# Two MLPs behind an attention: the first MLP's last eight output products as seven quarter products, and its scale and offset applied behind them

## The chip, the cores and the metric

The kernel runs on one core of a Trainium2 chip. The metric is device time in microseconds: before, the median of three runs is 846.16 (846.07 to 846.45).

## The reference

Sparse attention over 4 sequences of 576 tokens and 8 heads of 64 gives x of 2304 tokens by 512. Two MLPs follow, each of width 2048. All is float32, and the second MLP has its own weights.

```python
# first MLP                       # second MLP
h = x @ w_in                      h = x @ w_in
r = np.maximum(h, 0.0)            g = where(h >= 1, h, where(h <= -1, 0, (h + 1)**2 / 4))
g = s * (r * r) + b               out = g @ w_out
out = g @ w_out                   # s and b are one number each
```

## The kernel before

**Engines.** PE is TensorE (matmuls), DVE is VectorE, ACT is ScalarE, POOL is GpSimd, SP is SyncE, which issues nearly all the DMAs.

**Number format.** Each float32 matrix is split into a high and a low part (fp32r), and each product is three matmuls: high by high, high by low, low by high (`mm3` at L698 to L700, `mm3s` at L948 to L950). The high part is a copy on ACT (`copy`, L311), the low part a subtraction on DVE. Weights arrive as 64-bit floats, 128 rows of 512 numbers (0.52 MB) each, and `decode` turns them to float32: one ACT step (L329) and two DVE steps (L331, L333).

**First MLP.** The tokens are six units of 384 (`UNITS`), the width 16 blocks of 128 (index g). `hidden(g, u)` makes one block for one unit: 12 matmuls into PSUM tile `h` (two of them), relu on ACT (L720), square on ACT or DVE (L724, L726), s and b (`affine`: DVE at L733, ACT at L731), the high part `gh` (L311) and the low part `gl` (L737). Two steps later `output(u, g)` adds this block's share to four accumulators `acc0..3` in 12 more matmuls. A step is thus 24 matmuls of 384 columns. The list `segments` first goes through blocks 0 to 7 for all units; their sums are stored to DRAM (`part_d`). Then blocks 8 to 15 follow unit by unit, and the last addition (L775) adds the stored half and leaves x2, the second MLP's input. The attention of later tokens runs between the steps of units 0 to 4. Unit 5 with blocks 0 to 7 ends at about 283 us, the first MLP at about 491 us.

**Second MLP.** Pairs of units are multiplied by seven products of quarters (`PRODS`) in place of eight; `SUMS` lists the sums of token quarters, T1 to T4, and the matching sums S1 to S4 of weight quarters are made beforehand by `prepare(o, i)`: two blocks decoded, four sums (L392), the seven quarters split (L311, L377) and stored to DRAM as `dw` (eight stores, on SP). There are 16 such calls, each once. `inputs(p)` makes the sums and splits of a pair's x2 (L815, L834); `hidden2(p)` and `output2(p)` hold the matmuls, six to a block, and load one 262 KB quarter of weights (`wmat`, L871) per block.

**Order of the work.** `Issue.order` plans it: each operation has a duration by engine, its dependencies and a due time worked backward from the end. The planner always starts what can start first, then what is due first, and every engine runs its operations in that order. A tag with a count (`buf`) is a ring of buffers: an operation that needs one waits for the oldest to be free. The planner prices a DMA by `DMA_RATE`, 390 GB/s.

## Time and profile before

| | |
|---|---|
| median of three runs | 846.16 us |
| profiled execution | 847.01 us |
| its span, first to last instruction | 845.2 us |
| around the span | 1.8 us |
| mean granted TensorE clock | 0.983 |

A page shows one profiled execution. The busy share of PE is that of pipelined matmuls whose shown durations overlap, so its rate is read from the count of matmuls in a stretch. "Idle before" in a group of instructions says how long the engine stood before them and what ended it; it costs time only where that engine's work is on the chain that ended last.

### The profile page before, as it was taken

To read this page: it belongs to the slowest core of one execution; us is meant where nothing else is said; L and a number is where in the kernel's file an instruction comes from. 1 tells how busy PE (TensorE), PEld (TensorE's weight loads), DVE (VectorE), ACT (ScalarE), POOL (GpSimd) and SP (SyncE) were. 2 spreads that over 40 slices of the span, in tenths; PEclk is the share of its full clock that TensorE was granted. 3 is DMA by queue.
4 is the path that set the end of the run, shared out by engine and by line. 5 is a ranking of instruction groups with operands and counts; after the bars stand their busy time and mean duration, and the time that the engine had idled before them with its cause. 6 is when DMAs were issued, how large, how long until landed. Compare 5 with 4: busy or idle time off the path is not lost.

```text
span 845.2 us, 17439 instructions
## 1 busy us (share of the span) xinstructions
PE 822.4 (97%) x6338; PEld 799.1 (95%) x6338; DVE 595.7 (70%) x1247; ACT 519.3 (61%) x1093; POOL 22.9 (3%) x68
## 2 busy tenths in 40 slices
PE   7699999999999999999999999999999999999998
PEld 4479998989999899999999999999999999999998
DVE  3679637475698885767778356897666998465966
ACT  5467645554576774556667467875477855577653
POOL 2110000010000000000001000000000000000000
PEclk8689999999999999999999999999999999999999
DMA  8959272363389993768786457888987889888883
GB/s 245 270 172 287 98 241 66 92 181 108 122 283 329 293 304 128 226 220 259 261 293 203 151 181 244 264 254 267 290 275 254 254 252 289 293 252 253 254 263 105
DMA packets 115931, 191.78 MB, mean 227 GB/s; under 512 B 13830, under 2 KB 57990, under 8 KB 115846
## 3 DMA queue, kind: packets, MB, share of 16 engines
q1 hardware_dynamic: 114818, 190.23, 71.1%
q8 instruction: 51, 0.84, 0.4%
q10 hardware_dynamic: 1028, 0.43, 0.2%
q14 instruction: 34, 0.28, 0.1%
HBM read 150.25 MB, written 40.37 MB: 226 GB/s over the span
## 4 chain that ended last, share of the span: by engine, by line
PE 83%; DMA 9%; DVE 4%; ACT 2%; issue 2%; SPq 0%; ACTq 0%; DVEq 0%
PE h L698 6%; PE h L699 6%; PE acc L698 6%; PE h L700 6%; PE acc L699 6%; PE acc L700 6%; PE acc L949 6%; PE acc L948 6%; PE acc L950 6%; PE side L949 5%; PE side L948 5%; PE side L950 5%; DMA raw<-in_w_ins 4%; PE h L949 3%; PE h L950 3%; PE h L948 3%
## 5 line engine op out<-in xcount | busy, mean ns | idle before, releaser
L720 ACT ACTIVATE t<-h 128x384 f32<-128x384 f32 x96 | 46.5, 484 | 57.8 <-PE h L700 57.5
L698 PE MATMUL acc<-gh,w1hx 128*128 128x384 f32 x192 | 65.3, 340 | 0.4 <-ACT gh L311 0.4
L698 PE MATMUL h<-xh,w0hx 128*128 128x384 f32 x192 | 65.1, 339 | 0.0
L699 PE MATMUL acc<-gl,w1hx 128*128 128x384 f32 x192 | 64.9, 338 | 0.3
L699 PE MATMUL h<-xl,w0hx 128*128 128x384 f32 x192 | 64.5, 336 | 0.0
L700 PE MATMUL acc<-gh,w1lx 128*128 128x384 f32 x192 | 64.5, 336 | 0.0
L700 PE MATMUL h<-xh,w0lx 128*128 128x384 f32 x192 | 64.2, 334 | 0.0
L311 ACT ACTIVATE gh<-t 128x384 fp32r<-128x384 f32 x96 | 50.0, 520 | 23.0 <-DVE t L733 22.5
L737 DVE TENSOR_TENSOR gl<-t,gh 128x384 fp32r<-128x384 f32 x93 | 51.6, 555 | 16.4 <-ACT gh L311 16.2
L733 DVE TENSOR_SCALAR t<-t,fix_t 128x384 f32<-128x384 f32 x79 | 37.7, 477 | 35.2 <-ACT t L724 34.9
L698 PE MATMUL acc<-gh,w1h 128*128 128x384 f32 x168 | 57.0, 339 | 0.0
L699 PE MATMUL acc<-gl,w1h 128*128 128x384 f32 x168 | 56.4, 336 | 0.0
L700 PE MATMUL acc<-gh,w1l 128*128 128x384 f32 x168 | 56.3, 335 | 0.0
L698 PE MATMUL h<-xh,w0h 128*128 128x384 f32 x144 | 50.3, 349 | 0.1
L699 PE MATMUL h<-xl,w0h 128*128 128x384 f32 x144 | 49.3, 342 | 0.1
L700 PE MATMUL h<-xh,w0l 128*128 128x384 f32 x144 | 49.2, 342 | 0.1
L724 ACT ACTIVATE t<-t 128x384 f32<-128x384 f32 x81 | 42.4, 523 | 2.1
L699 PEld LDWEIGHTS acc<-gl,w1hx 128*128 128x128 f32 x192 | 36.0, 188 | 1.2 <-DVE gl L737 1.1
L698 PEld LDWEIGHTS acc<-gh,w1hx 128*128 128x128 f32 x192 | 36.0, 188 | 1.1 <-ACT gh L311 0.7
L698 PEld LDWEIGHTS h<-xh,w0hx 128*128 128x128 f32 x192 | 36.0, 188 | 0.3
L699 PEld LDWEIGHTS h<-xl,w0hx 128*128 128x128 f32 x192 | 36.1, 188 | 0.0
L700 PEld LDWEIGHTS h<-xh,w0lx 128*128 128x128 f32 x192 | 36.1, 188 | 0.0
(518 smaller groups left out, 2515.7 us busy)
## 6 DMA issues: line engine op xcount, KB each, us to landing
w0h<-dw SPq DMA_DIRECT2D x84, 256.0 KB
w0l<-dw SPq DMA_DIRECT2D x84, 256.0 KB
w0hx<-dw SPq DMA_DIRECT2D x84, 256.0 KB
w0lx<-dw SPq DMA_DIRECT2D x84, 256.0 KB
raw<-in_w_ins SPq DMA_DIRECT2D x32, 512.0 KB
raw<-in_w_outs SPq DMA_DIRECT2D x32, 512.0 KB
dw<-pt SPq DMA_DIRECT2D x48, 256.0 KB
dw<-po SPq DMA_DIRECT2D x48, 256.0 KB
```

The source lines that it names most:

```text
L311: e.activation(out=out, in_=in_, func=AF.Copy)
L698: e.matmul(out=acc, lhsT=wh, rhs=ah, start=first, stop=False)
L699: e.matmul(out=acc, lhsT=wh, rhs=al, start=False, stop=False)
L700: e.matmul(out=acc, lhsT=wl, rhs=ah, start=False, stop=last)
L720: op(lambda e: e.activation(out=c(t), in_=c(p), func=AF.Relu), [act(n)], [p], [t])
L724: e.activation(out=c(t), in_=c(t), func=AF.Square)
L733: e.tensor_scalar(out=c(t), in0=c(t), scalar1=sb_t[:, 0:1], scalar2=sb_t[:, 1:2], op0=MUL, op1=ADD)
L737: op(lambda e: e.tensor_tensor(out=c(gl), in0=c(t), in1=c(gh).bitcast(F32), op=SUB), [pool(n)] + [dve2(n)], [t, gh], [gl])
L948: e.matmul(out=dst, lhsT=wh, rhs=ah, start=opens and first, stop=False, skip_group_check=not opens)
L949: e.matmul(out=dst, lhsT=wh, rhs=al, start=False, stop=False, skip_group_check=not opens)
L950: e.matmul(out=dst, lhsT=wl, rhs=ah, start=False, stop=last, skip_group_check=not opens)
```

## The change

- `affine` is taken out of `hidden`. As g = s r² + b, the first MLP's output is s (r² W) + b times the column sums of W. Both are applied once, behind the sums, by 24 ACT operations in `second_steps` (`last`).
- The column sums come from the matmuls: for unit 2 in the first half (`COUNTED`), and for three of the seven products of pair 0 in the second, the token operand gets two more columns, one of ones and one of zeros (`units`, on POOL), and `column` reads the result.
- The output products of blocks 8 to 15 are done for pairs of units as seven products of quarters (`first_steps`, `second_steps`, `product`), each of four blocks of six matmuls. `first_steps(p)` makes the hidden blocks of a pair without a split, 16 of them; `second_steps(p)` runs the 28 product blocks, among which the hidden blocks of the next pair are spread.
- W's last eight blocks go through `prepare` (o = 2, four calls) in place of `weights`: 20 calls in all. Nine now come in the first half, from unit 1 on (`AT_FIRST`), ten in the second half (`AT_HALF`), one in the second MLP (`AT_NEXT`). A call's parts are stored high and low together, in four DMAs issued by POOL, from a ring `pp` of two buffers.
- Several operations lose POOL as an alternative, buffers change places, and `place` and `G_TAGS` use other tags.

```diff
+RAW, DT, KB, QV, SM, PT, PP, TB = 3, 2, 4, 3, 3, 2, 2, 3
...
-EARLY = 6
+KQ = MS // 2
+AT_FIRST = {(1, 6): 1, (2, 0): 1, (2, 3): 1, (2, 6): 1, (3, 1): 1, (3, 4): 1, (3, 7): 1, (4, 2): 1, (4, 5): 1}
+AT_HALF = {(0, 0): 1, (0, 2): 1, (0, 5): 1, (0, 7): 1, (1, 1): 1, (1, 3): 1, (1, 5): 1, (1, 7): 1, (2, 1): 1, (2, 3): 1}
+AT_NEXT = {0: 1}
...
+S_TAGS = ["kb"] * 4 + ["qx", "sx"]
+SPLIT, SUMMED, SUM_BACK, EVAC2 = (0.0, 6.0, 6.0), (0.0, 0.0, 0.0), 0, 5.0
+RAW_LAG, STORE_LAG = 3.0, 4.0
+COUNTED = 2
...
+    mask_t = sp.tile([128, 1024], F32, name="mask_t", tag="pp", bufs=PP)[:, 0:64]
...
+    half_t, pre_t, ones_t, sums_t = few_t[:, 0:1], few_t[:, 1:2], few_t[:, 2:6].bitcast(F32R), few_t[:, 6:]
...
+    counts = (KP, KP, KQ)
+    dw = [[dr.tile([7, 128, 2, 256], F32, name=f"dw{o}_{i}") for i in range(n)] for o, n in enumerate(counts)]
...
+    def decode(src, after=(), allocs=(), t=None, line=None, raw=None):
+        late = RAW_LAG if raw else 0.0
+        raw = raw or buf(sp, "raw", [128, 2 * DM], I32, RAW)
         t = t or buf(sp, "dt", [128, DM], I32, DT)
...
+        q_, d_, lag_ = dma(src.shape[0] * src.shape[1] * 8)
+        load = op(lambda e: e.dma_start(out=raw.tile.bitcast(I64), in_=src), [(q_, d_, lag_ + late)],
                   writes=[raw], after=after, allocs=allocs, line=line)
...
+    STORE = lambda nq: ("pool", 1.0, STORE_LAG)
+
+    def prepare(o, i, early=False):
+
         src = w_outs if o else w_ins
-        at = o * KP + i
-        tag = ("qv", "sm")[at % 2]
-        d1, d2 = (buf(sp, tag, [128, DM], I32, BUFS[tag]) for _ in range(2))
-        _, x1, _, load = decode(src[2 * MS + i], lasts if at < EARLY else [*lasts, chain[0]], [d1, d2], d1)
-        _, x2, *_ = decode(src[2 * MS + KP + i], [load], (), d2)
+        base = MS if o == 2 else 2 * MS
+        begin, at = len(plan.ops), len(prepared)
+        tag = "dt" if early else ("qv", "sm")[at % 2]
+        d1, d2 = (buf(sp, tag, [128, DM], I32, DT if early else BUFS[tag]) for _ in range(2))
+        r1, r2 = (buf(sp, "raw", [128, 2 * DM], I32, RAW) for _ in range(2))
+        _, x1, _, load = decode(src[base + i], [chain[0]] if early else [*lasts, chain[0]], [r1, r2], d1, p_line, r1)
+        _, x2, *_ = decode(src[base + counts[o] + i], [load], (), d2, p_line, r2)
...
-            n, q = 256 * len(names), [WMAT[name] for name in names]
+            nq, q = len(names), [WMAT[name] for name in names]
             qs = slice(q[0], q[-1] + 1, max(q[-1] - q[0], 1))
-            hi = buf(sp, "pt", [128, 512], F32R, PT)
-            lo = buf(sp, "po", [128, 512], F32R, PO)
-            x = lambda: f()[:, k * 256:k * 256 + n]
-            op(lambda e: copy(e, hi.tile[:, 0:n], x()), [act(n)], [b], [hi], allocs=[lo])
-            op(lambda e: e.tensor_tensor(out=lo.tile[:, 0:n], in0=x(), in1=hi.tile[:, 0:n].bitcast(F32), op=SUB),
-               [pool(n), dve2(n)], [b, hi], [lo])
-            for w, y in enumerate((hi, lo)):
-                op(lambda e, y=y, w=w: e.dma_start(
-                    out=dw[o][i][qs, :, w, :].rearrange("q p n -> p q n"),
-                    in_=y.tile[:, 0:n].bitcast(F32).rearrange("p (q n) -> p q n", n=256)), [dma(n * 512)], [y],
-                   part=[dw_buf[o][i][v] for v in q])
+            y = buf(sp, "pp", [128, 2, 2, 256], F32R, PP)
+            x = lambda: f()[:, k * 256:(k + nq) * 256].rearrange("p (q n) -> p q n", n=256)
+            op(lambda e: copy(e, y.tile[:, 0:nq, 0, :], x()), [act(256 * nq)], [b], [y])
+            op(lambda e: e.tensor_tensor(out=y.tile[:, 0:nq, 1, :], in0=x(), in1=y.tile[:, 0:nq, 0, :].bitcast(F32), op=SUB),
+               [dve2(256 * nq)], [b], [y])
+            op(lambda e: e.dma_start(out=dw[o][i][qs].rearrange("q p w n -> p q (w n)"),
+                                     in_=y.tile[:, 0:nq].bitcast(F32).rearrange("p q w n -> p q (w n)")),
+               [STORE(nq)], [y], part=[dw_buf[o][i][v] for v in q])
 
...
+    def hidden(g, u, whole=None):
         n = UNITS[u]
         p = buf(ps, "h", [128, UMAX], F32, 2)
-        t = buf(sp, "t", [128, UMAX], F32, TB)
-        gh = buf(sp, "gh", [128, UMAX], F32R, LAG + 1)
-        gl = buf(sp, "gl", [128, UMAX], F32R, LAG + 1)
+        if whole:
+            t, own = whole, [whole]
+        else:
+            t = buf(sp, "t", [128, UMAX], F32, TB)
+            more = 2 * (u == COUNTED)
+            gh = buf(sp, "gh", [128, UMAX + more], F32R, LAG + 1)
+            gl = buf(sp, "gl", [128, UMAX + more], F32R, LAG + 1)
+            own = [t, gh, gl]
         w = wt[g, 0]
         for k in range(KD):
             pe_op(lambda e, k=k: mm3(e, p.tile[:, 0:n], cut(w, k), (xh[u][:, k, :], xl[u][:, k, :]), k == 0, k == KD - 1),
-                  n, [*w, x_buf[u][k]], [p], [t, gh, gl] if k == 0 else ())
+                  n, [*w, x_buf[u][k]], [p], own if k == 0 else ())
         x_last[u] = chain[0]
...
         op(square, [act(n), dve2(n), pool(n)], (), [t])
-        def affine(e):
-            if e is nc.scalar:
-                e.activation(out=c(t), in_=c(t), func=AF.Identity, scale=sb_t[:, 0:1], bias=sb_t[:, 1:2])
-            else:
-                e.tensor_scalar(out=c(t), in0=c(t), scalar1=sb_t[:, 0:1], scalar2=sb_t[:, 1:2], op0=MUL, op1=ADD)
-
-        op(affine, [act(n + 200), dve2(n, 0.00084)], [fix_buf], [t])
+        if whole:
+            return
         op(lambda e: copy(e, c(gh), c(t)), [act(n)], [t], [gh])
         op(lambda e: e.tensor_tensor(out=c(gl), in0=c(t), in1=c(gh).bitcast(F32), op=SUB),
            [pool(n)] + [dve2(n)], [t, gh], [gl])
+        if more:
+            units(gh, gl, n)
         return gh, gl
+
+    def units(hi, lo, n):
+        op(lambda e: [copy(e, b.tile[:, n:n + 2], ones_t[:, v:v + 2]) for b, v in ((hi, 0), (lo, 2))], [("pool", 0.4, 0.1)],
+           part=[hi, lo], after=[*hi.writers, *lo.writers])
+
+    bias_sum = Buf(None, None)
+
+    def column(src, c, at, opens):
+        one = lambda: src.tile[:, NP:NP + 1]
+        to = sums_t[:, at:at + 1]
+        op(lambda e: e.tensor_copy(out=to, in_=one()) if opens else e.tensor_tensor(out=to, in0=one(), in1=to, op=ADD),
+           [("dve", 0.15, 0.1)], [src], part=[bias_sum], after=() if opens else bias_sum.writers)
...
-    def output(u, m, g, gt, opens, closes, earlier, last):
+    def output(u, m, g, gt, opens, closes, earlier):
         n = UNITS[u]
         w = wt[g, 1]
-        cg = lambda: tuple(b.tile[:, 0:n] for b in gt)
+        z = n + 2 * (u == COUNTED)
+        cg = lambda: tuple(b.tile[:, 0:z] for b in gt)
...
             if opens:
-                acc[c] = buf(ps, f"acc{c}", [128, UMAX], F32, 1)
+                acc[c] = buf(ps, f"acc{c}", [128, z], F32, 1)
             a = acc[c]
-            pe_op(lambda e, a=a, c=c: mm3(e, a.tile[:, 0:n], cut(w, c), cg(), opens, closes), n, [*w, *gt], [a])
+            pe_op(lambda e, a=a, c=c: mm3(e, a.tile, cut(w, c), cg(), opens, closes), n, [*w, *gt], [a])
         if not closes:
             return
         line = []
         for c in range(KD):
             a = acc[c]
-            if last:
-                y = pin[c]
-                op(lambda e, y=y, a=a, c=c: e.tensor_tensor(out=x2[u].tile[:, c, :], in0=a.tile[:, 0:n], in1=y.tile[:, 0:n],
-                                                            op=ADD),
-                   [dve(n)], [a, y], part=touched(u, c), allocs=[x2[u]] if c == 0 else (), line=line).sooner = EVAC
-                continue
+            if u == COUNTED:
+                column(a, c, c, True)
...
-                op(sums, [("dve", 0.07 * len(todo) + 2 * NP * 0.00104, 0.1, "port"),
-                          ("pool", 0.1 * len(todo) + 2 * NP * 0.0022, 0.1, "port")],
+                op(sums, [("dve", 0.09 * len(todo) + 2 * NP * 0.00104, 0.1, "port")],
...
+            home_ = f"xl{i}" if i < NU else f"xh{2 * p + 1}"
+            ring = rings.setdefault(("T", home_), Ring(1))
+            ring.name = f"T{home_}"
...
+            op(lambda e, src=src, hi=hi: [copy(e, h(), s()) for s, h in zip(src, hi)],
+               [("act", 0.17 * n + 2 * NP * 0.00062, 0.1)], [quarter[p][place]], [b],
+               after=[x_last[i], *(mixed if i < 2 else ())] if i < NU else plan.ops[begin:])
+            op(lambda e, src=src, hi=hi, lo=lo: [e.tensor_tensor(out=l(), in0=s(), in1=h().bitcast(F32), op=SUB)
+                                                 for s, h, l in zip(src, hi, lo)],
+               [("dve", 0.09 * n + 2 * NP * 0.00104, 0.1, "port")],
+               [quarter[p][place]], [b])
...
+        if o == 2:
+            tag = S_TAGS[loads[1] % len(S_TAGS)]
+            y = buf(sp, tag, [128, 2, 256], F32R, BUFS[tag])
+        else:
+            tag = ("w0h", "w0l", "w0hx", "w0lx")[loads[0] % 4]
+            y = buf(wp, tag, [128, 2, 256], F32R, MS // 2)
+        loads[o == 2] += 1
...
+    def product(o, k, a, b, g_of, dst, counted=False):
+        for i in range(counts[o]):
+            home = b
+            if b in SUMS:
+                home, l, r = SUMS[b]
+                d, l, r = (g_of[i, v] for v in (home, l, r))
+                op(lambda e, d=d, l=l, r=r: e.tensor_tensor(out=d.tile, in0=l.tile, in1=r.tile, op=SUB),
+                   [dve2(n)], [v for v in (l, r) if v is not d], [d], after=sum_after(o)).sooner = SUMMED[o]
+            g = g_of[i, home]
+            z = n + 2 * counted
+            deep = o == 2 and len(blocks) % (LAG + 2) == LAG + 1
+            hi = buf(sp, "pt" if deep else "gh", [128, z], F32R, PT if deep else LAG + 1)
+            lo = buf(sp, "pt" if deep else "gl", [128, z], F32R, PT if deep else LAG + 1)
+            op(lambda e, g=g, hi=hi: copy(e, hi.tile[:, 0:n], g.tile), [act(n)], [g], [hi], allocs=[lo], line=g_line)
+            op(lambda e, g=g, hi=hi, lo=lo: e.tensor_tensor(out=lo.tile[:, 0:n], in0=g.tile, in1=hi.tile[:, 0:n].bitcast(F32), op=SUB),
+                   [dve2(n)], [g, hi], [lo]).sooner = SPLIT[o]
+            if counted:
+                units(hi, lo, n)
+            w = wmat(o, i, a)
+
+            def f(e, dst=dst, w=w, hi=hi, lo=lo, k=k, i=i):
+                for c in range(2):
+                    wc = [w.tile[:, v, c * 128:(c + 1) * 128] for v in range(2)]
+                    mm3s(e, dst[c].tile[:, 0:z], wc, (hi.tile, lo.tile), k in START, i == 0, i == counts[o] - 1)
+
+            pe_block(f, [w, hi, lo], dst)
+            blocks.append(chain[0])
+            yield
+
+    halves, spares, mixed = [{} for _ in range(PAIRS)], {}, []
+
+    def spare(tag):
+        if tag not in spares:
+            spares[tag] = const.tile([128, KD, NP], F32, name=f"g_{tag}", tag=tag)
+        return spares[tag]
+
+    def inner(p, m, u):
+        if p != 1:
+            return buf(wp, ("w1h", "w1l")[u % 2] + ("" if m < KQ else "x"), [128, n], F32, MS // 2)
+        j = 2 * m + u % 2
+        if j < 2 * KD:
+            return Part(lambda: spare(f"xl{j // KD}")[:, j % KD, :])
+        tag = (["pi"] * KD + ["t"] * TB + ["dt"])[j - 2 * KD]
+        return buf(sp, tag, [128, n], F32, {"pi": KD, "t": TB, "dt": DT}[tag])
+
+    def first_steps(p):
+        us = (2 * p, 2 * p + 1)
+        for g in range(MS, 2 * MS):
+            m = g - MS
+            make(0, g + 1)
+            for u in us:
+                y = halves[p][m % KQ, f"B{m // KQ + 1}{u % 2 + 1}"] = inner(p, m, u)
+                hidden(g, u, y)
+                if pend:
+                    output(*pend.pop(0))
+                yield
+            for _ in range(AT_HALF.get((p, m), 0)):
+                prepare(*todo.pop(0))
+
+    def second_steps(p):
+        us, affine = (2 * p, 2 * p + 1), []
+        slot = {u: [Buf(None, None) for _ in range(KD)] for u in us}
+        for u in us:
+            op(lambda e, u=u: e.dma_start(out=x2[u].tile, in_=part_d[u].rearrange("c p n -> p c n")), [dma(KD * n * 512)],
+               part_buf[u], slot[u], after=[x_last[u]], allocs=[x2[u]])
+        sets = [[buf(ps, t, [128, NP + 2 * (p == 0)], F32, 2 if t == "side" else 1) for t in ts]
+                for ts in (("side", "side"), ("acc0", "acc1"), ("acc2", "acc3"))]
+        x, z, y = sets[p % 3:] + sets[:p % 3]
+        for k, a, b in PRODS:
+            dst = {1: x, 6: x, 7: x, 4: x, 5: z, 3: z, 2: y}[k]
+            counted = p == 0 and k in START
+            yield from product(2, k, a, b, halves[p], dst, counted)
+            r, t, ends = {1: (1, 0, 0), 5: (2, 1, 0), 6: (1, 1, 0), 3: (1, 1, 1), 7: (2, 1, 1), 2: (1, 0, 1), 4: (2, 0, 1)}[k]
+            u = us[t]
+            for c in range(2):
+                j = c + 2 * (r - 1)
+                d = slot[u][j]
+                op(lambda e, u=u, j=j, s=dst[c]: e.tensor_tensor(out=x2[u].tile[:, j, :], in0=s.tile[:, 0:n], in1=x2[u].tile[:, j, :],
+                                                                 op=ADD),
+                   [dve(n)], [dst[c]], [d]).sooner = EVAC2
+                if counted:
+                    column(dst[c], c, KD + c + 2 * (k == 5), k != 2)
+            if counted and k == 2:
+                op(lambda e: e.tensor_tensor(out=sums_t[:, 0:KD], in0=sums_t[:, 0:KD], in1=sums_t[:, KD:], op=ADD), [("dve", 0.15, 0.1)],
+                   writes=[bias_sum])
+                op(lambda e: e.tensor_scalar(out=sums_t[:, 0:KD], in0=sums_t[:, 0:KD], scalar1=sb_t[:, 1:2], scalar2=None, op0=MUL),
+                   [("dve", 0.15, 0.1)], [fix_buf], [bias_sum])
+                for a_ in affine:
+                    a_()
+            if ends:
+                for c in range(2):
+                    j = c + 2 * (r - 1)
+
+                    def last(u=u, j=j):
+                        op(lambda e: e.activation(out=x2[u].tile[:, j, :], in_=x2[u].tile[:, j, :], func=AF.Identity,
+                                                  scale=sb_t[:, 0:1], bias=sums_t[:, j:j + 1]),
+                           [act(n + 200)], [fix_buf, bias_sum], [slot[u][j]], part=touched(u, j))
+
+                    if p == 0 and not k in (2, 4):
+                        affine.append(last)
+                    else:
+                        last()
+
...
+            if u == NU - 1:
+                make(0, MS + g + 1)
+            for _ in range(AT_FIRST.get((u, g), 0)):
+                prepare(*todo.pop(0), early=u < NU - 1)
...
     x0_free = []
+    list(first_steps(0))
+    for p in range(PAIRS):
+        more, done_, step = first_steps(p + 1) if p + 1 < PAIRS else iter(()), 0, 0
+        for _ in second_steps(p):
+            step += 1
+            while done_ < step * 2 * MS / (7 * KQ):
+                next(more, None)
+                done_ += 1
+        list(more)
+        if p == 1:
+            mixed.append(chain[0])
+    assert len(todo) == sum(AT_NEXT.values())
```

## Rows read from the trace of the kernel before

**Rows 1.** The page's first part: busy time, share of the span, instructions by engine.

```profile
PE 822.4 (97%) x6338; PEld 799.1 (95%) x6338; DVE 595.7 (70%) x1247; ACT 519.3 (61%) x1093; POOL 22.9 (3%) x68
```

**Rows 2.** Windows: stretch, its length; busy time by engine; granted clock, DMA share, GB/s.

```profile
44.00:110.00 66.00, 64.30 (x690) 59.64 (x689) 52.53 (x118) 45.90 (x100) 3.32 (x6) 0.97 0.60 191
110.00:230.00 120.00, 119.75 (x1530) 111.96 (x1529) 71.52 (x183) 59.91 (x131) 5.86 (x20) 1.00 0.41 125
...
250.00:283.00 33.00, 33.00 (x192) 32.89 (x191) 27.62 (x58) 23.27 (x48) 0.00 (x0) 1.00 0.98 317
283.00:320.00 37.00, 34.56 (x192) 32.89 (x191) 31.40 (x65) 28.07 (x57) 0.00 (x0) 1.00 0.87 278
340.00:840.00 500.00, 500.00 (x2881) 499.88 (x2880) 361.93 (x699) 316.12 (x625) 5.41 (x5) 1.00 0.77 246
...
260.00:270.00 10.00, 10.00 (x59) 10.00 (x58) 8.32 (x19) 7.88 (x17) 0.00 (x0) 1.00 0.99 336
...
540.00:560.00 20.00, 20.00 (x117) 20.00 (x116) 19.51 (x37) 16.96 (x35) 0.00 (x0) 1.00 0.80 255
```

**Rows 3.** Waits from 278 to 322: who waited for whom, us, times, longest.

```profile
PE acc L698 <- ACT pi L311: 1.8, 1, 1.8
PEld acc L699 <- DVE gl L737: 1.3, 4, 0.4
```

**Rows 4.** The chain of waits from 44 to 72: start, length, what.

```profile
53.76 0.35 DVE t L733
...
66.64 0.40 DVE t L733
...
69.41 0.44 PE h L699
```

**Rows 5.** Groups of instructions, whole span: busy, mean ns of one, idle before.

```profile
L720 ACT ACTIVATE t<-h 128x384 f32<-128x384 f32 x96 | 46.5, 484 | 57.8 <-PE h L700 57.5
L311 ACT ACTIVATE gh<-t 128x384 fp32r<-128x384 f32 x96 | 50.0, 520 | 23.0 <-DVE t L733 22.5
L737 DVE TENSOR_TENSOR gl<-t,gh 128x384 fp32r<-128x384 f32 x93 | 51.6, 555 | 16.4 <-ACT gh L311 16.2
L733 DVE TENSOR_SCALAR t<-t,fix_t 128x384 f32<-128x384 f32 x79 | 37.7, 477 | 35.2 <-ACT t L724 34.9
L724 ACT ACTIVATE t<-t 128x384 f32<-128x384 f32 x81 | 42.4, 523 | 2.1
...
L377 DVE TENSOR_TENSOR po<-sm,pt 128x512 fp32r<-128x512 f32 (+1 forms) x32 | 19.8, 623 | 4.0 <-ACT pt L311 2.8 <-ACT dt L329 1.1
...
L311 ACT ACTIVATE pt<-sm 128x512 fp32r<-128x512 f32 (+1 forms) x32 | 18.4, 574 | 8.8 <-DVE sm L392 4.4 <-DVE sm L333 2.7 <-DMA dw<-pt 1.2
...
L834 DVE TENSOR_TENSOR tm<-x,tm 128x768 fp32r<-128x768 f32 x18 | 17.0, 954 | 0.6 <-ACT tm L311 0.6
...
L775 DVE TENSOR_TENSOR x<-acc,pi 128x384 f32<-128x384 f32 x24 | 12.2, 553 | 3.5 <-PE acc L700 3.5
...
L731 ACT ACTIVATE t<-t,fix_t 128x384 f32<-128x384 f32 x17 | 12.0, 705 | 0.5
...
L333 DVE SCALAR_TENSOR_TENSOR sm<-raw,sm 128x512 int32<-128x512 int32 x16 | 11.0, 688 | 0.2
...
L329 ACT ACTIVATE sm<-raw 128x512 f32<-128x512 f32 x16 | 10.6, 665 | 14.3 <-DMA raw<-in_w_outs 8.4 <-DMA raw<-in_w_ins 5.8
```

**Rows 6.** Groups on DVE from 320 to 480: two steps of a weight's preparation.

```profile
L392 DVE TENSOR_TENSOR qv<-qv,qv 128x256 f32<-128x256 f32 x13 | 5.5, 423 | 0.2
...
L331 DVE TENSOR_SCALAR sm<-sm 128x512 int32<-128x512 int32 x10 | 4.3, 427 | 9.8 <-ACT sm L329 9.8
```

**Rows 7.** Groups on POOL, whole span: a small copy.

```profile
L313 POOL COPY q<-xl 128x36 f32<-128x36 f32 x6 | 1.2, 211 | 7.1 <-DMA xl<-in_strd 7.0
```

**Rows 8.** Who waited for the DMAs of tile dw: us in total, times.

```profile
  ACT pt L311: 2.0, 5
```

**Rows 9.** The chain of waits from 264 to 276: a store's landing.

```profile
270.18 4.22 DMA dw<-pt
```

More of the change, by code (lines that the diff above doesn't have):

```diff
@@ L71 @@
 DMA_ISSUE = 0.45
[L72 removed]
+BY_SLOT, ACC_ACT = 3, 0.38
 class Buf:
@@ L81, in __init__ @@
         self.tile, self.left, self.end, self.near = None, 0, 0.0, 0.0
+class Part(Buf):
+    def __init__(self, at):
+        super().__init__(None, None)
+        self.at = at
+    tile = property(lambda self: self.at(), lambda self, t: None)
 class Ring:
@@ new lines, in inputs @@
+            home_ = f"xl{i}" if i < NU else f"xh{2 * p + 1}"
+            ring = rings.setdefault(("T", home_), Ring(1))
+            ring.name = f"T{home_}"
+            b = Buf(ring, lambda i=i, p=p, home_=home_: const.tile([128, 2, 2, NP], F32R, name=f"tm{p}_{i}", tag=home_))
+            bufs = [b]
+            at = lambda w, j, b=b: b.tile[:, w, j, :]
+            whole = lambda w, d, n, b=b: b.tile[:, w, :, d:d + n]
+            hi = [lambda d=d, n=n, f=whole: f(0, d, n) for _, _, d, n in pieces]
@@ new lines, in inputs @@
+            lo = [lambda d=d, n=n, f=whole: f(1, d, n) for _, _, d, n in pieces]
+            n = len(pieces)
+            op(lambda e, src=src, hi=hi: [copy(e, h(), s()) for s, h in zip(src, hi)],
[5 more added lines that the diff above has]
+               [quarter[p][place]], [b])
@@ L936, in nonlinear @@
         in_psum = what == "C21"
-        op(lambda e: e.activation(out=t.tile, in_=c.tile, func=AF.Relu, scale=0.5, bias=half_t), [act(n)], [c], [t])
+        op(lambda e: e.activation(out=t.tile, in_=c.tile, func=AF.Relu, scale=0.5, bias=half_t), [act(n)], [c], [t],
+           after=sum(prepared, []) if p == 0 and tag in ("qv", "sm", "pt") else ())
         op(lambda e: e.activation(out=t.tile, in_=t.tile, func=AF.Square), [act(n)], (), [t])
@@ L957, in hidden2 @@
             cs = [{}, {}]
+            for _ in range(AT_NEXT.get(i0, 0) if p == 0 else 0):
+                prepare(*todo.pop(0))
             for k, a, b in PRODS:
@@ L1037, in sparse_attention_two_mlps @@
     for u, g0, g1 in segments:
-        earlier, last = seen[u] > 0, g1 == 2 * MS
+        earlier = seen[u] > 0
         seen[u] += 1
@@ L1042, in sparse_attention_two_mlps @@
         for g in range(g0, g1):
-            hf, m = divmod(g, MS)
             make(0, g + 1)
-            pend.append((u, m, g, hidden(g, u), g == g0, g == g1 - 1, earlier, last))
+            pend.append((u, g, g, hidden(g, u), g == g0, g == g1 - 1, earlier))
             make(1, g + 1 - LAG)
```

149 lines of the change are left out of this document (35 added, 114 removed).

## The prediction

> **What bounds the kernel now.** I read the busy shares first, then windows by stage, then the waits and the chain of waits where a window fell short. The busy shares show PE at 97%, DVE at 70%, ACT at 61% [rows 1]. The windows say where the rest is: from 340 to 840 PE never stands, and 2881 matmuls in 500 us make 0.1736 us for one [rows 2]. The same pace gives 192 x 0.1736 = 33.3 us for the first half's last unit, which took 33.0 (250 to 283) [rows 2]. Two places fall short. From 283 to 320 the same 192 matmuls took 37 us, PE standing 37 - 34.56 = 2.4 us by its busy time and 3.7 by its count [rows 2]; the reader sees PE wait there for ACT's copy of an accumulator and for DVE's `gl` [rows 3], while DVE is 85% busy and the DMA engines 87% to 98% [rows 2]. Decoding of the second half's weights causes it. And from 53 to 69 the chain leaves PE for DVE [rows 4]. Elsewhere the end is set by the number of matmuls.
>
> **The change part by part.**
>
> *Matmuls.* Output products of blocks 8 to 15 are now 8 x 2 x 12 = 192 matmuls for a pair, afterwards 28 blocks x 6 = 168. Three pairs save 72, x 0.1736 = 12.5 us, on the path in full. The added columns: 96 matmuls of unit 2 and 3 x 4 x 6 = 72 of pair 0 carry 386 columns for 384; at 0.1736/384 = 0.00045 us a column that is 168 x 2 x 0.00045 = 0.15 us. Sum -12.35.
>
> *Affine gone, in the first half.* 79 on DVE at 0.477 and 17 on ACT at 0.705 go [rows 5]; 24 come on ACT, behind the sums. Only where DVE or the latency of a step is on the chain does this show: two pieces there, 0.35 + 0.40 [rows 4]. Between 0 (the next DVE operation is as late) and three whole ones, 1.4. I take -0.75, the chain's own two pieces.
>
> *The burst at 283.* Before, sixteen second-half weights and six preparations met there. Afterwards the first half's last unit has eight decodes, and the preparations lie earlier or later. What is late next is ACT, with `h` to drain every 2.08 us. Between 0 and -3.7; I take -2.4, PE's idle time.
>
> *Preparations in the first half.* One costs DVE 2 x (0.427 + 0.688) + 4 x 0.423 + 4 x 0.623 = 6.4 us and ACT 2 x 0.665 + 4 x 0.574 = 3.6 [rows 5, 6]. From about 112 to 250 nine come. In the 120 us from 110 DVE was busy 71.5 [rows 2]; some 25 steps lose 0.477 x 79/96 each, -10; eight of the nine add 51. That is 113 of 120, 94%. ACT goes from 60 to 89. DMA: a call loads 1.05 MB and stores 7 x 0.262 = 1.84, so eight bring 23 MB to the 125 GB/s x 120 us = 15 there; 38 MB in 120 us are 317 GB/s, where the best ten microseconds had 336 [rows 2]. Both are near their limits; a call that slips falls into the last unit's 33 us, which lost some twenty decodes. The cover is the attention's lead; without it PE stands as at 283, 2.4 in 37, so 7.8 in 120. At the other end stands 540 to 560, DVE 19.51 of 20 and PE unbroken [rows 2]. I take +1.5, nearer to the latter.
>
> *Second half.* `first_steps(0)`: 192 matmuls, 33.3 us, four preparations: DVE 26, ACT 16 x (0.484 + 0.523) + 14.5 = 31 [rows 5], of which squares can move to DVE. Then twice 28 x 1.04 + 33.3 = 62.5 us with both kinds of blocks, then 29.2 us of product blocks alone. A pair's products cost DVE 28 splits, 16 sums and 14 additions, 58 x 0.555 = 32.2 us [rows 5]. With pair 0 come four preparations, 32.2 + 25.7 = 57.9 of 62.5, ACT 14.6 + 16.1 + 14.5 + 8 x 0.705 = 50.8. DVE again is 93% full; between 0 and the rate of 283, 4.1. I take +1: preparations for `output2` have slack of a stage. The second 62.5 us hold 45 of DVE, which is covered.
>
> *Into the second MLP.* The first sums T lie in buffers free only when pair 1's products are done, so they fall into pair 2's, when no hidden blocks are left. DVE needs 32.2 there; about four splits (2.2) run ahead, as many as buffers allow. The operands of the first three products add 0.95 + 1.9 + 1.9 = 4.8 [rows 5], due 29.2 + 4.2 = 33.4 after the stage begins: 34.8 of work, 1.4 late. With nothing ahead it is 32.2 + 4.8 - 29.2 = 7.8; with more ahead 0. I take +1.5, the sum.
>
> *Stores from POOL.* The trace of before has no DMA issued by POOL. ACT waited 2.0 us in five waits on the old stores [rows 8], 128 of them; one landed in 4.2 us [rows 9]. Now 80 go through two buffers. The planner puts ACT's next copy 5 us behind, so nothing waits if that holds. Between 0 and the rival below; I take +0.3, less than what ACT waited. `units` puts some 0.2 us a copy [rows 7] between `gl` and PE, under a lead of two steps, 8 us; without that lead 0.4 x 20 = 8.
>
> The Trainium skill, "SBUF — State Buffer", section "SBUF: two separate sides", speaks against this edit: a DMA issued by GpSimd cannot write its descriptors while VectorE runs an operation in a two-port mode. Here only the 512-element shift at 0.427 us runs faster than one element per nanosecond [rows 6], two in a preparation, so by that page a store starts up to 0.43 us later, 40 times; the planner's lead covers it and the sum stays. No run before shows such a store.
>
> Sum: -12.35 - 0.75 - 2.4 + 1.5 + 1 + 1.5 + 0.3 = -11.2. The profiled execution's own time is 847.0 (span 845.2 and 1.8 around it), so 835.8; the median of the runs lies 0.85 lower, so 835.0.
>
> **The rivals.**
>
> 1. *ACT stands behind the stores (slower).* A store that lands more than some 5 us after its split holds ACT's copy into the ring of two; relu and `gh` are queued behind it, and PE stands when both `h` tiles are full. For: ACT already waited on stores [rows 8], and DMA is fuller now. Against: two tiles and 13 us from call to call. At one hold of 0.75 us on PE per preparation, 20 of them, it adds 15: 850.0. It decides from 0.56 us a call, where the 11.2 are gone. The page named above tells of a store of about 0.6 us that took 3.1 beside VectorE's copies; by that, as an estimate, landings of 4.2 would become 6.7, beyond the planner's 5.
> 2. *DVE is the bound into the second MLP.* Nothing runs ahead, 7.8 in place of 1.5: 841.3. For: work and span nearly equal. Against: 540 to 560 [rows 2].
> 3. *The first half fills up.* DVE at 94% and DMA at 317 GB/s delay attention tiles and PE stands, 7.8 in place of 1.5: also 841.3. For: the planner counts 390 GB/s, the chip gave 336 [rows 2]. Against: preparations can slip.
> 4. *All cover holds.* -12.35 - 3.7 - 1.4 and no new stall: 828.7. For: the 500 us from 340 show PE unbroken, 540 to 560 with DVE full [rows 2].
>
> That the saving fails to arrive is no case: the matmuls are fewer by count and PE has no slack after 340.
>
> **How the numbers follow.** Forecast 0.45, all cover holds 0.22, DVE 0.12, first half 0.12, stores 0.09. The time is the forecast's, 835.0. The range goes from the best case's 828.7, a little under it for a rounding of its terms, to beyond the two at 841.3: 828.0 to 844.0; it leaves out the stores and the case of two stalls together. 0.2%, 1.7 us, is what a measurement of this kernel can tell from no change. Slower is the stores' case, 0.09; 0.04 is for stalls that add up to the saving; faster 0.87.
>
> **What would show it.** Right: 72 matmuls fewer; 2881 matmuls per 500 us from the second half on, with at most some 5 us lost; the first MLP ending about 11 us earlier; no wait on `dw` above a few microseconds in total. Wrong: PE waiting for `gl` or for a tile of the second MLP at its start (rival 2); for `xl` or an attention tile between 110 and 250, with DMA near 330 GB/s there (rival 3); ACT waiting on stores, with relu late behind it (rival 1). No hole at all would bring the fourth. A start of PE's matmuls moved from 44 us would be a step I have not priced.

## The result and the profile after

The changed kernel takes 837.77 us in the median of four runs (835.43 to 838.07), the kernel before 846.12 beside it (845.75 to 846.45): a ratio of 0.9895 [0.9877, 0.9914]. That is 8.35 us less, where 11.2 were forecast. Two later repeats beside fresh runs of the kernel before gave 0.9936 and 0.9945, some 5 us less (experiments e1 and e9). The profiled execution is the fastest of the four: 835.43, its span 833.6.

The first part of the page of the changed kernel, which answers to [rows 1]:

```profile
PE 809.8 (97%) x6263; PEld 788.5 (95%) x6263; DVE 627.3 (75%) x1335; ACT 526.5 (63%) x1120; POOL 92.3 (11%) x186
```

DVE has gained 32 us and POOL 69. PE still works for 97% of a shorter span. For where the time went, the starts of the matmuls of 384 or 386 columns say more than shares: the trace of before has 4320 of them, that of after 4248, 72 fewer. Cut at three of these starts, the two profiles give (worked out from the traces; us):

| stretch | before | after | difference |
|---|---|---|---|
| span's start to the first hidden matmul | 44 | 40 | -4.4 |
| A: from there to the second half's first hidden matmul | 238.9 | 243.3 | +4.4 |
| B: from there to the second MLP's first matmul | 208.7 | 195.0 | -13.7 |
| C: the second MLP's matmuls | 349.6 | 351.8 | +2.2 |

A, B and C together are 7.1 shorter. The first line can't be put down to the change: the kernel before, run with tiles a few bytes wider and the same order of work (e4), began at 40 too, and other versions at 41 to 45. In the chain before that start, PE stands in three pieces of 5.5 us together for nothing that the profile shows ("issue") in the profile of before, 2.4 in e4's, none to speak of in this one. Whether that is the execution's or the program's is not shown; four profiles of the changed kernel (this one, e1, e2, e9) begin at 39.7 to 41.0, and of the unedited kernel before there is one. So four of the 11.6 us that the two spans differ by are kept out of the account; the 8.35 of the medians lies between 7.1 and 11.6.

The windows of the changed kernel, with the columns of [rows 2]:

```profile
44.00:110.00 66.00, 64.20 (x729) 60.32 (x728) 49.60 (x113) 43.54 (x100) 3.71 (x11) 1.00 0.66 205
110.00:230.00 120.00, 115.22 (x1442) 107.25 (x1442) 92.18 (x241) 65.44 (x142) 29.76 (x58) 1.00 0.74 251
230.00:283.00 53.00, 53.00 (x306) 53.00 (x305) 35.46 (x69) 31.53 (x63) 8.80 (x13) 1.00 0.69 239
283.00:320.00 37.00, 37.00 (x215) 37.00 (x215) 23.73 (x47) 25.94 (x52) 7.02 (x14) 1.00 0.67 229
283.00:480.00 197.00, 195.38 (x1117) 194.80 (x1117) 156.97 (x325) 133.12 (x266) 35.07 (x62) 1.00 0.85 290
520.00:545.00 25.00, 25.00 (x145) 24.84 (x144) 24.11 (x45) 21.27 (x44) 1.43 (x2) 1.00 0.91 306
545.00:565.00 20.00, 20.00 (x116) 20.00 (x115) 19.25 (x37) 12.23 (x26) 0.00 (x0) 1.00 0.78 242
```

Three things are to be seen. From 283 to 320, where PE had lost 2.4 us, it now works without a break, with DVE at 24 us in place of 31. From 110 to 230 it stands for 4.8 us, where it had stood for 0.25 with DVE at 72 and DMA at 125 GB/s. Into the second MLP, whose first matmul comes at 478, it never stands, with DVE 96% busy from 520 to 565.

PE's waits in the changed kernel from 110 to 300 (what waited for what, us, times, longest):

```profile
PE side L580 <- DMA kb<-in_strd: 3.2, 2, 2.6
PE h L636 <- DVE sx L627: 1.5, 1, 1.5
```

The chain of waits of the changed kernel at the first of them (start, length, what), an attention tile that lands late:

```profile
161.81 6.95 DMA kb<-in_strd
168.80 0.62 PE side L580 x32
...
171.51 5.95 DMA kb<-in_strd
177.50 0.62 PE side L580 x32
```

And at the second, the first rival's chain in full:

```profile
205.70 8.38 DMA dw<-pp
...
214.16 0.64 ACT pp L328
...
215.44 0.68 DVE pp L391
...
218.11 0.69 DVE sx L627
...
218.94 0.63 PE h L636 x4
```

A store issued by POOL lands after 8.38 us, twice the 4.22 of [rows 9]; ACT's next copy into the ring waits for it, DVE's split for that, an attention step stands behind the split, and PE waits 1.5. Who waited for these stores in the whole span, the line that answers to [rows 8]:

```profile
ACT pp L328 <- DMA dw<-pp: 36.9, 27, 4.6
```

Five waits of 2.0 us in all have become 27 of 36.9. Nearly all is idle time of an engine that has slack; 1.5 reached PE by the chain above. The stores themselves, from the DMA issues (count, size, median us from issue to landing):

```profile
dw<-pp POOLq DMA_DIRECT2D x60, 512.0 KB, 4.9
dw<-pp POOLq DMA_DIRECT2D x20, 256.0 KB, 4.7
```

The second half loses 1.6 us at one place. PE's waits from 283 to 480:

```profile
PE side L952 <- ACT gh L328: 1.3, 1, 1.3
PE side L952 <- DMA kb<-dw: 0.3, 1, 0.3
```

The smaller part is a tile of product operands from DRAM, the larger ACT's copy `gh`, in the chain of the changed kernel:

```profile
443.55 7.48 DMA kb<-dw
451.16 0.41 PE side L952
...
452.49 0.43 ACT x L1079
...
453.33 0.42 ACT gh L328
453.75 0.41 PE side L952
```

Ahead of `gh` ACT runs two of the new scale and offset operations (`x`, L1079), and just before these, from 448 to 451, it had stood 1.4 us for two stores. Which of the two the 1.3 us are owed to is not shown.

That leaves the second MLP, whose matmuls the change does not touch and which is 2.2 us longer without a wait of PE. Its six stages, hidden and output in turn, take 58.3, 58.5, 58.3, 58.2, 58.3, 58.1 before and 58.3, 59.2, 58.2, 59.0, 58.3, 58.9 after: every output stage has grown, no hidden stage has.

### The profile page after: what moved, and what is told of

Same layout as the page of the kernel before. It is cut to its first block, busy times and chain, and to the rows that moved or that the text cites. A ratio compares the mean times of both kernels' runs of the same rounds, so it can differ in the third digit from the quotient of the medians.

```text
span 833.6 us, 17675 instructions
## 1 busy us (share of the span) xinstructions
PE 809.8 (97%) x6263; PEld 788.5 (95%) x6263; DVE 627.3 (75%) x1335; ACT 526.5 (63%) x1120; POOL 92.3 (11%) x186
## 3 DMA queue, kind: packets, MB, share of 16 engines
q0 software_dynamic: 10240, 36.71, 11.6%
## 4 chain that ended last, share of the span: by engine, by line
PE 89%; DMA 6%; DVE 2%; issue 1%; ACT 1%; SPq 0%; POOL 0%; ACTq 0%; POOLq 0%
PE acc L954 8%; PE acc L953 8%; PE acc L952 8%; PE h L709 8%; PE h L710 7%; PE h L711 7%; PE side L952 6%; PE side L953 6%; PE side L954 6%; PE acc L709 4%; PE h L954 3%; PE h L953 3%; PE h L952 3%; PE acc L710 3%; PE acc L711 3%; DMA kb<-in_strd 2%
## 5 line engine op out<-in xcount | busy, mean ns | idle before, releaser
L393 POOL DMA_DIRECT2D dw<-pp x80 | 55.1, 690 | 273.2 <-DVE pp L391 198.6
L711 PEld LDWEIGHTS h<-xh,w0l 128*128 128x128 f32 x192 | 36.3, 189 | 1.0 <-DVE w0l L364 1.0
L709 PEld LDWEIGHTS h<-xh,w0h 128*128 128x128 f32 x192 | 36.4, 190 | 0.5
L710 PEld LDWEIGHTS h<-xl,w0h 128*128 128x128 f32 x192 | 36.3, 189 | 0.3 <-DVE xl L692 0.3
L348 ACT ACTIVATE dt<-raw 128x512 f32<-128x512 f32 x42 | 27.7, 667 | 9.2 <-DMA raw<-in_w_ins 6.8
L709 PE MATMUL acc<-gh,w1hx 128*128 128x384 f32 (+1 forms) x96 | 33.4, 348 | 0.0
L709 PE MATMUL acc<-gh,w1h 128*128 128x384 f32 (+1 forms) x96 | 33.2, 346 | 0.0
L711 PE MATMUL acc<-gh,w1lx 128*128 128x384 f32 (+1 forms) x96 | 32.4, 338 | 0.0
L710 PE MATMUL acc<-gl,w1hx 128*128 128x384 f32 (+1 forms) x96 | 32.4, 338 | 0.0
L711 PE MATMUL acc<-gh,w1l 128*128 128x384 f32 (+1 forms) x96 | 32.4, 337 | 0.0
```

The costliest lines, as they stand in the source:

```text
L348: first = op(lambda e: e.activation(out=x(), in_=words(1).bitcast(F32), func=AF.Prelu, scale=2.0 ** -112, alpha=-2.0 ** 32), [act(DM)], [r ...
L393: op(lambda e: e.dma_start(out=dw[o][i][qs].rearrange("q p w n -> p q (w n)"), in_=y.tile[:, 0:nq].bitcast(F32).rearrange("p q w n -> p q ...
L709: e.matmul(out=acc, lhsT=wh, rhs=ah, start=first, stop=False)
L710: e.matmul(out=acc, lhsT=wh, rhs=al, start=False, stop=False)
L711: e.matmul(out=acc, lhsT=wl, rhs=ah, start=False, stop=last)
```

## The experiments

The theory after the first comparison: the matmuls are saved in full; the columns of ones cost more than their own pass, because every tile of the rings `gh` and `gl` has become 386 columns wide and an output matmul that reads such a tile is slower (in the built program the tiles lie 1568 bytes apart in a partition, before 1536); and the preparations of the first half cost more than priced. The rivals: that the second MLP is slower through DMA traffic, and that the stores from POOL are the whole loss of the first half.

**e1, the changed kernel again**, with no edit, as the measure for the runs beside it.

> The changed kernel once more, untouched, as the measure for the others and for what its runs differ by. Its four runs so far lie between 835.4 and 838.1, where the kernel before keeps within 0.7. Theory A (addresses): the high and low parts gh and gl became 386 columns wide, so their tiles start 1544 bytes apart in place of 1536, and PE reads them slower: in the second MLP the matmuls of output2 take 0.1755 us each in place of 0.1735, those of hidden2 0.1734 as before. Theory B (something else makes output2 slower: the order of the splits, where its inputs lie) expects the same of this run. Both: 837.5, second MLP 2.2 us longer than before.

Measured: 839.55 against 844.49, 0.9936 [0.9912, 0.996]. A 245.5, B 196.6, C 351.7. Runs of both kernels spread more here than in the first comparison (before 842.3 to 851.1), so totals that differ by 2 us say little and the lengths of stretches say more. The gain is smaller than in the first comparison. The profile has it in A and B, 2.2 and 1.6 longer than in the first one; why is not settled.

**e2, tiles of 392 columns** (`WIDE = 392`) in the rings `gh` and `gl`, here and in `product`.

```diff
-            gh = buf(sp, "gh", [128, UMAX + more], F32R, LAG + 1)
+            gh = buf(sp, "gh", [128, WIDE], F32R, LAG + 1)
...
```

> The changed kernel with the tiles of gh and gl made 392 columns wide (1568 bytes, a multiple of 32), of which the matmuls read the same 384 or 386 columns. Nothing else is touched. Theory A: output2's matmuls come back to 0.1735 us, the second MLP gets 2.2 us shorter, the first MLP's output matmuls give another 1: about 834.3. If only multiples of 64 do, it gives less. Theory B: no difference, 837.5.

Measured: 838.70, 0.9924 [0.9899, 0.9948]; C 351.8. The edit was void: in the built programs 386 columns were already laid out as 392, so every tile has the address it had. It is a third run of the changed kernel and says nothing on width.

**e3, no columns of ones.** The column sums are set to zero, so b is left out.

```diff
-COUNTED = 2
+COUNTED = -1
...
-        sets = [[buf(ps, t, [128, NP + 2 * (p == 0)], F32, 2 if t == "side" else 1) for t in ts]
+        sets = [[buf(ps, t, [128, NP], F32, 2 if t == "side" else 1) for t in ts]
...
-            counted = p == 0 and k in START
+            counted = False
...
```

> The changed kernel without the columns of ones: gh and gl have 384 columns again, the 168 matmuls of 386 columns have 384, the POOL copies of ones and DVE's readings of the sums are gone. It leaves b out of the result (the offset is set to 0). Theory A: 834.3, with output2 at 0.1735 us a matmul. Theory B: the two columns cost 0.15 us in all and the small operations lie beside other work: 837.3.

Measured: 840.17, 0.9932 [0.991, 0.9954]; A 247.1, B 199.8, C 349.8. The second MLP is back at its length before, with output stages of 58.8, 58.2 and 58.1. The total is none of the two expected ones: it has not moved, as the planner made another order, in which PE waits at other places. PE's waits in e3 from 110 to 480:

```profile
PE h L636 <- DVE sx L627: 4.1, 1, 4.1
PE side L952 <- DMA kb<-dw: 2.4, 1, 2.4
PE side L650 <- DVE sm L619: 2.2, 1, 2.2
PE h L709 <- ACT g_xl L736: 1.9, 1, 1.9
```

So the run settles C and leaves the total of the columns open. It shows too that an order planned anew shifts several microseconds of waits by itself.

**e4, the kernel before with wide tiles**: nothing of the change but two unused columns behind each `gh` and `gl`.

```diff
-        gh = buf(sp, "gh", [128, UMAX], F32R, LAG + 1)
-        gl = buf(sp, "gl", [128, UMAX], F32R, LAG + 1)
+        gh = buf(sp, "gh", [128, UMAX + 2], F32R, LAG + 1)
+        gl = buf(sp, "gl", [128, UMAX + 2], F32R, LAG + 1)
...
```

> The kernel before with the tiles of gh and gl made 386 columns wide, of which it uses 384. Nothing else is touched. Theory A: output2's 1008 matmuls take 2 ns more each, 2.2 us, and the first MLP's 1152 output matmuls up to 2.5: 849.5. Theory B: no difference, 846.1.

Measured: 848.91 against 844.49, 1.0046 [1.0026, 1.0065]. A is longer by 0.9, B by 0.9, C by 2.1; the output stages take 59.1, 59.0 and 58.8. No matmul has more columns and the engines run the same operations in the same order, so the tiles' places alone do it. One output stage's window in four kernels, in this order the one before, after, e3 and e4:

```profile
670.00:720.00 50.00, 50.00 (x290) 49.94 (x290) 43.97 (x86) 28.85 (x57) 0.00 (x0) 1.00 0.86 270
```

```profile
657.00:707.00 50.00, 50.00 (x287) 50.00 (x286) 43.41 (x85) 28.76 (x57) 0.00 (x0) 1.00 0.85 267
```

```profile
668.00:718.00 50.00, 50.00 (x290) 50.00 (x289) 43.27 (x86) 28.64 (x56) 0.00 (x0) 1.00 0.88 271
```

```profile
668.00:718.00 50.00, 50.00 (x286) 50.00 (x286) 43.76 (x86) 28.66 (x57) 0.00 (x0) 1.00 0.86 266
```

PE works all 50 us at full clock in each, with 290 matmuls at a spacing of 1536 bytes and 286 or 287 at 1568. DMA differs by 5 GB/s and goes neither with the one nor with the other, so the rival with DMA falls. Worked out from the starts, a matmul on `gh` or `gl` in the second MLP follows the one before it after 173.5 to 173.6 ns in the kernel before, 175.3 to 175.9 in e4 and 174.9 to 176.3 in the changed kernel, one on `tm` after 173.4 to 173.5 in all of them. In A and B, waits left out, one on `gh` follows after 175.0 and 175.2 in e4, for 173.7 and 174.3 before.

**e5, tiles of 400 columns**, 1600 bytes apart, a multiple of 64 (`WIDE = 400`, in the same places); a constant moves to another tile to make room.

```diff
-            gh = buf(sp, "gh", [128, UMAX + more], F32R, LAG + 1)
+            gh = buf(sp, "gh", [128, WIDE], F32R, LAG + 1)
...
```

> The changed kernel with gh and gl tiles 400 columns wide (1600 bytes, a multiple of 64). The room comes from the first 96 columns of fix_t, used at the start alone, which go into a buffer of the ring pp, by a DMA of their own. Theory A, in the form that multiples of 64 bytes decide (392 columns gave nothing): output2 at 0.1735 us a matmul, the second MLP 349.6 in place of 351.8, another 1 in the first MLP: 3 us under the changed kernel. If it is something else in the two columns, the second MLP stays at 351.8.

Measured: 839.36 against 846.84, 0.993 [0.9905, 0.9954]; C 351.2, with output stages of 59.4, 58.6 and 58.4. The first has four gaps at operands that are split late, 0.7 us together; without them it is 58.7. So all three lie between the 58.1 and the 59.2 of the kernels before and after, and a part comes back. A window of e5 in the same stage holds 289 matmuls:

```profile
668.00:718.00 50.00, 50.00 (x289) 50.00 (x288) 42.61 (x84) 27.63 (x55) 0.00 (x0) 1.00 0.84 269
```

A multiple of 64 bytes is then not all that it takes. What in the address decides stays open; 1536 is the only spacing of these two rings seen at full pace.

**e6, the preparations late**: four calls in the first half in place of nine, fifteen in the second in place of ten (`AT_HALF`).

```diff
-AT_FIRST = {(1, 6): 1, (2, 0): 1, (2, 3): 1, (2, 6): 1, (3, 1): 1, (3, 4): 1, (3, 7): 1, (4, 2): 1, (4, 5): 1}
+AT_FIRST = {(4, 2): 1, (4, 5): 1, (5, 0): 1, (5, 3): 1}
...
```

> The changed kernel with four preparations in the first half (units 4 and 5) in place of nine, and fifteen in place of ten in the second half. Theory C: the preparations in the first half cost it 4.4 to 6.6 us (from the first hidden matmul to the second half's first, 243.3 and 245.5 in two profiles, 238.9 before). Then this stretch comes back to about 239.5. The second half holds five more, some 32 us of DVE, and 14 MB: up to 5 us longer. Total between 5 less and the same as the changed kernel. Rival (the first half is longer for another reason, its order): 243 to 245 as before.

Measured: 880.16, 1.0414 [1.0375, 1.0454]; A 238.7, B 195.6, C 395.6. The first half is as short as before, with no wait of PE from 110 to 300. So its loss is the preparations', their stores included, as far as one run with an order of its own can show it. Windows of e6 there and into the second MLP:

```profile
110.00:230.00 120.00, 120.00 (x1473) 112.56 (x1472) 58.55 (x154) 55.29 (x119) 11.36 (x39) 1.00 0.38 120
476.00:640.00 164.00, 130.05 (x690) 124.33 (x689) 129.43 (x256) 98.11 (x195) 19.75 (x29) 0.89 0.87 320
```

What left the first half is paid for many times over: fifteen calls in the second half end too late and the weights of the second MLP with them. PE's waits in e6 from 476 to 640:

```profile
PE side L952 <- ACT gh L328: 10.5, 1, 10.5
PE side L952 <- DMA w0hx<-dw: 10.0, 1, 10.0
PE side L953 <- DVE gl L999: 4.7, 1, 4.7
```

**e7, the stores on SP's queue**, the order planned anew with the price of any other DMA.

```diff
-    STORE = lambda nq: ("pool", 1.0, STORE_LAG)
+    STORE = lambda nq: dma(nq * 1024 * 256)
```

> The changed kernel with the preparations' 80 stores issued by SP in place of POOL. Theory D: a store issued by POOL lands late for its descriptors (one took 8.4 us, planned 5), ACT waited 36.9 us for the ring of two and DVE behind it 1.5 us on PE's path. Then ACT's wait on stores falls below 15 us and the total by 1 to 2. Rival: the stores land late because the DMA engines are full, whoever issues them; ACT's wait stays, SP's queue holds loads up besides: the same or up to 3 slower.

Measured: 836.17 against 846.84, 0.9893 [0.9857, 0.9929]; A 241.4, B 194.9, C 351.9. The total fell as expected, but ACT's waits for stores did not: they were to fall below 15 us, and only the longest is shorter, 2.8 for 4.6.

```profile
ACT pp L328 <- DMA dw<-pp: 32.9, 31, 2.8
```

**e8, an order planned with a slower DMA**, 300 GB/s for 390 and 8 us for a store's landing.

```diff
-RAW_LAG, STORE_LAG = 3.0, 4.0
+RAW_LAG, STORE_LAG = 3.0, 8.0
...
-DMA_RATE = 390.0e3
+DMA_RATE = 300.0e3
```

> The changed kernel planned with 300 GB/s in place of 390 and with 8 us in place of 4 for a store's landing. Only the order of the work changes. Theory C in the form that the plan believes in DMAs faster than they are: waits of PE on kb and of ACT on stores get rare, 2 to 4 us less in the first half. Rival: DMA and DVE are full in any order: within 1 us of the changed kernel.

Measured: 898.66, 1.0619 [1.0578, 1.0661]; A 274.9, C 382.1. PE's waits in e8 from 200 to 330 are one:

```profile
PE h L709 <- ACT w0h L328: 27.3, 1, 27.3
```

The second half's first weights are ready 27 us late; the chain before that wait runs through the preparations' stores, one after the other until 306, with the split and the decode behind the last. A slower price made the order worse. That it pushes whole preparations past their stage, as the stages are packed so closely, is a reading of that chain and was not tested.

**e9, the changed kernel again, and e10, the stores on SP again**, measured side by side.

> The changed kernel untouched, as the measure for the next two on the same chip: 837 to 840. Both theories expect the same: stretch from the first hidden matmul to the second half's first 243 to 245.5, PE waiting 3 us there for kb.

> The stores on SP once more, beside the changed kernel on one chip. Theory D (POOL's stores land late for how they are issued): 2 to 3 below the changed kernel in the median, ACT's longest wait for a store under 3 (2.8 in the run before, 4.6 with POOL), the first half 241.4. Rival (the two are one, the earlier difference was between runs): within 1.

Measured against 844.62: 839.43, 0.9945 [0.9927, 0.9963] for e9; 836.85, 0.9912 [0.9879, 0.9945] for e10, 2.6 us less in the median, the intervals overlapping. A is 246.3 in e9 and 240.0 in e10; the second MLP's first output stage takes 60.5 and 59.9, for 59.2 in the first profile, with PE waiting for late splits in both. ACT's waits for stores are 35.6 us in e9, the longest 3.8, and 20.9 in e10, the longest 2.6. The windows from 110 to 230, e9 and then e10:

```profile
110.00:230.00 120.00, 115.06 (x1432) 107.02 (x1431) 89.89 (x235) 63.32 (x138) 29.04 (x58) 0.99 0.72 244
```

```profile
110.00:230.00 120.00, 118.87 (x1464) 111.13 (x1463) 92.44 (x236) 66.73 (x142) 13.98 (x39) 1.00 0.75 250
```

With as much DVE work and as much traffic, PE loses 1.1 us in place of 4.9. PE's waits in e10 from 110 to 300:

```profile
PE side L580 <- DMA kb<-in_strd: 0.9, 1, 0.9
PE side L650 <- ACT pt L328: 0.2, 1, 0.2
```

Of the first half's loss most goes with the stores' queue. The orders of the two kernels are not the same, so a part may be the order's.

**e11, e10's edit and seven calls in the first half**, twelve in the second.

```diff
-AT_FIRST = {(1, 6): 1, (2, 0): 1, (2, 3): 1, (2, 6): 1, (3, 1): 1, (3, 4): 1, (3, 7): 1, (4, 2): 1, (4, 5): 1}
+AT_FIRST = {(1, 6): 1, (2, 2): 1, (2, 6): 1, (3, 2): 1, (3, 6): 1, (4, 2): 1, (4, 5): 1}
...
```

> Stores on SP, and seven preparations in the first half with twelve in the second, in place of nine and ten. Theory C (the calls in the first half cost it some 0.6 each, and the second half has room): first half 240, second half 195, the second MLP as before the move: 1 to 2 below the run with SP's stores alone. Rival (as with four and fifteen the last calls come too late): the second MLP waits for dw at its start or at output2's, 5 to 40 slower.

Measured: 842.33, 0.9971 [0.9952, 0.9989]; A 239.7, B 194.2, C 361.7. Two calls fewer save 0.3 in A over e10; the first output stage takes 69.0, where PE waits for operands split late. PE's waits in e11 from 470 to 600:

```profile
PE side L952 <- ACT gh L328: 4.7, 1, 4.7
PE side L953 <- DVE gl L999: 1.4, 3, 0.7
```

**e12, the kernel before without `affine`**; s and b are left out.

```diff
-        op(affine, [act(n + 200), dve2(n, 0.00084)], [fix_buf], [t])
```

> The kernel before with affine taken out and nothing in its place; it leaves s and b out of the result. Theory of the prediction: 0.75 less in the start and, DVE having 38 us less, some of the 2.4 to 3.7 lost at 283: 1 to 3 below before. Rival: affine lay wholly beside PE's work: within 0.5 of before.

Measured: 846.67 against 844.62, 1.0024 [1.0006, 1.0042]. A is 240.4, B 206.9, C 349.6. B is 1.8 shorter, A 1.5 longer. Both theories miss. Taking 96 operations from DVE and ACT gave nothing in the total; why it is slightly longer stays open, as the order is planned anew here too.

The shortest version found is the changed kernel with its stores on SP's queue (e7, e10): 836.17 and 836.85, with 846.84 and 844.62 for the kernel before beside them.

## Why the prediction was right, and where its sizes were not

The direction and the mechanism were right, and the time lies in the range: 837.8 for 835.0. The saving was 8.35 us for 11.2; in the two later repeats it was 4.9 and 5.2, less than half of the forecast. Point by point:

1. **Matmuls: -12.5 held, +0.15 for the columns did not.** 72 are gone, and B is shorter by 13.7, of which 72 x 0.1735 = 12.5. The step that failed is the term for the columns: "The added columns: 96 matmuls of unit 2 and 3 x 4 x 6 = 72 of pair 0 carry 386 columns for 384". I counted the matmuls that carry the columns; the cost lies on all that read a ring of wider tiles. In C it is 2.2. e4 shows 0.9 each for A and B, and B has seven output matmuls for eight, so 0.8 as an estimate; a quarter of these read another ring, `pt`, so it is rather less. Together 3.9 in place of 0.15: by the first profile the largest error of the sum. That such tiles alone make the kernel slower is shown by e4, and that C returns without them by e3.
2. **Preparations in the first half: +1.5 was too small, and the stores' +0.3 too.** A grew by 4.4, of which 0.9 is point 1: 3.5 for 1.8. In the later profiles of the changed kernel A is 245.5, 243.8 and 246.3 (e1, e2, e9), so the term goes up to 6.6, against the one profile of before. PE waited for attention tiles (rival 3) and once for the chain of a late store (rival 1), 4.7 us in all. e6 shows that the preparations cause it, e7 and e10 that most goes with POOL's queue. So both rivals happened, at a fraction of their prices: 1.5 of PE's time for all stores' waits in this stretch, where rival 1 asked for 0.75 at each of 20 calls. "No wait on `dw` above a few microseconds in total", a sign named for being right, did not hold: ACT's were 36.9. The planner's 5 us for a landing was near the median of 4.9; the landings far above it were what counted. DVE came to 92 us of 120 and DMA to 251 GB/s, less than my 113 and 317: by the starts of the stores six of the nine calls lie in these 120 us, not eight. The other three slipped into the last unit, before 283, none into the second half, and PE still lost 4.8.
3. **Affine: -0.75 was not seen.** e12 has no gain in the total. The first 480 matmuls of 384 or 386 columns take 108.8 us before, 108.3 in e12 and 107.8 to 109.1 in four profiles of the changed kernel. So half a microsecond may be in it, which the executions differ by anyway. It lies near the end named for it, nothing; that the next DVE operation is as late is not shown.
4. **The burst at 283, -2.4, and the second half, +1: about right.** PE stands nowhere from 283 to 320, where [rows 3] had its waits, and 1.6 is lost at 451, for the most part behind ACT, where DVE was named. Without the 12.5 of the matmuls and the 0.8 of point 1, B is shorter by 2.0, for 1.4 forecast.
5. **Into the second MLP: 0 for +1.5.** PE never waits from 476 to 640, and hidden blocks and sums run with DVE at 96%. Rival 2 falls as a loss of 7.8; but in e9 the same kernel loses 1.5 in C at splits that come late, which is the size forecast, so 0 holds for the first profile alone. e6 and e11 show how near the rival lies: two more calls in the second half lengthen the first output stage from e10's 59.9 to e11's 69.0.

Put together: -12.5 + 3.9 + 3.5 - 2.0 = -7.1, which is what A, B and C show. The forecast's -11.2 is off by errors of both signs: 3.75 and 1.7 too little cost, 0.75 of gain that wasn't seen, against 1.5 and 0.6 that went better. That they cancel by a third is luck, and it helped the total. The 4.4 us earlier start in the profile belongs to none of them; the prediction named such a move as a step not priced.

Of the Trainium skill's page "SBUF — State Buffer", section "SBUF: two separate sides", the prediction took a store kept waiting by VectorE's work, with landings of 6.7 as an estimate. The median of 4.9 lies nearer to the 4.22 of before; single ones reached 8.9. The trace does not put the late ones down to VectorE. Two windows of the changed kernel, 3 us each from the issue of a store that landed after 8.38 us and of one that landed after 3.26:

```profile
205.70:208.70 3.00, 3.00 (x19) 3.00 (x19) 2.87 (x7) 0.83 (x2) 1.29 (x2) 1.00 0.89 295
215.80:218.80 3.00, 1.60 (x10) 1.27 (x8) 3.00 (x9) 2.59 (x6) 1.45 (x2) 1.00 0.53 199
```

DVE is busy in both; DMA is fuller in the first. So it is over all 80 stores (worked out from the trace): in the 3 us behind the issue of the 20 that landed soonest, after 2.3 to 3.9 us, DVE was busy 75% of the time and the packets of other queues took 18% of the DMA engines; for the 20 that landed last, after 6.1 to 8.9, it was 77% and 77%. Late landings go with full DMA engines and not with DVE's busy share; that DVE adds nothing at all is not shown. What makes SP's queue better in the first half (e7, e10) stays open, as the order differs with the issuer.

## What to carry to other kernels

A column added to an operand changes the size of its tile, and with it where every buffer of that ring lies: price it on all the instructions that read the ring, and look at a stage that the change does not touch. When the planner's price of a transfer is near the median landing, the late landings decide: look at what is queued behind the engine that waits for them. And compare profiles by stretches between the same instructions: here the start of the matmuls lay 4 us apart in two kernels with the same order of work (before and e4).
